# Two-layer gated MLP behind windowed attention on one core: layer 1's last 1024 tokens times w_out by seven block products, layer 2's w_in blocks stored in fp32

## The chip, the core and the metric

The kernel runs on one core of one Trainium2 chip. Time is what the device takes for one execution, in microseconds (us); several executions are timed and their median is given. The core's engines are TensorE (PE, the matrix engine; PEld is its weight load), the Vector engine (DVE), the Scalar engine (ACT), GpSimd (POOL) and SyncE (SP), which here issues nearly all DMA transfers. SBUF is the on-chip memory, PSUM holds what PE writes.

## The reference

2304 tokens pass through windowed attention (4 batches, 8 heads, 576 positions, head width 64, each query sees itself and the 63 keys before it) and then through two MLPs:

```python
x = attention(q, k, v)                       # (2304, 512)
h = x @ w_in1;  g = h - np.tanh(h)           # (2304, 2048)
x = (g @ w_out1).astype(np.float32)          # (2304, 512)
h = x @ w_in2;  g = h * (1.0 / (1.0 + np.exp(-1.702 * h)))
return (g @ w_out2).astype(np.float32)
```

The weights come as fp64; q, k and v as fp32. w_in is 512 x 2048, w_out 2048 x 512.

## The kernel before

**Accuracy.** Each fp64 weight is turned on chip into an fp32 number, and every fp32 operand of a product is split into a high half that PE's fp32r format holds exactly and a low half, the difference. A product is then three matmuls, hi x hi, hi x lo and lo x hi; the function `three` (L697) issues them. Multiplying one 128x128 weight tile so by 512 columns is 3 matmuls, and the weight loads go with them.

**Conversion.** A weight tile of 128x512 fp64 numbers is loaded as pairs of 32-bit words (`raw`). ACT takes the absolute value of the upper word (L305), DVE clamps it from below (L309), masks and shifts it (L312), puts in the bits of the lower word (L318) and the sign (L324); ACT writes the high half (L334), DVE the low half (L338). For layer 1 both halves stay in SBUF in one tile per f (f counts 16 columns of 128 of d_ff), w_in's part and w_out's side by side. For layer 2 `plan_wd` converts the tiles in pairs, POOL makes four sums S1 to S4 of their blocks (`wd_sums`, L380), ACT and DVE split plain blocks and sums alike (L384, L389), and both halves are stored to device memory (`wd_store`, L398): `wd` for w_in, `wdo` for w_out. They are fetched again later, as `ws` (`load_ws`, L440) and `wo` (`load_wo`, L444).

**Layer 1.** Tokens go in blocks of 512, 512, 256, 512 and 512 (0 to 4). For a block there are 16 steps h and 16 steps p, alternating with a lag of 2: step h (`hid`) multiplies x by one 128-column tile of w_in into the PSUM tile `psh` (4 x 3 = 12 matmuls, 512 columns each); ACT makes tanh and DVE subtracts (L723), ACT takes the high half gh and DVE the low half gl (L731); step p (`proj`) adds g times one row tile of w_out into four PSUM tiles `acc` (12 matmuls). At the end of a block the sums are evicted (`os`) and stored to device memory (`xs`), as layer 2 needs tokens in another grouping. Attention (L554 to L632) is spread over the first part of this.

**Layer 2.** Its first 256 tokens go the same way (a plain block). The other 2048 go in two units of 1024, u = 0 and 1, in which both matrix products are made with 7 block products in place of 8 (Winograd's form): sums and differences of blocks of the weights (S1 to S4) and of the activations (T1 to T4) are multiplied, and the seven products P1 to P7 are combined by additions on DVE. Tokens (two halves of 512) and the other side (pairs of tiles, j = 0 to 7) are the halves that the blocks are made from. The order of the products and the blocks that they take:

```python
PROD = dict(P1=(A11, "C11"), P5=(S1, "T1"), P6=(S2, "T2"), P7=(S3, "T3"), P2=(A12, "C21"), P3=(S4, "C22"), P4=(A22, "T4"))
OSEQ = (("P1", "P5", "P6", "P7", "P2", "P3", "P4"), ("P1", "P5", "P6", "P7", "P3", "P4", "P2"))
```

The gates of a unit lie in tiles `ug` (four parts of 512 columns per j: C11, C12, C21, C22); T1 to T4 are made from them by `u_sub` (L940, T1 on POOL, the others on DVE), split by `o_hi` (ACT, L950) and `o_lo` (DVE, L954) into gh and gl and multiplied with `ws` tiles into the PSUM tiles `ob` (`o_prod`). The unit's x side is `xt`, split into `xh`, `xl` or `xu` (L883, L890); `x2b` is the second partial of an x (L879).

**What sets the order.** No loop of the program is the order on the engines. Every piece of work is entered in a plan with its engine, an assumed duration, a due time (`prio`), what it waits for and which slots of a pool it takes and gives back (`raw` 3, `gp` 3, `psh` 2, `ws` 4, ...). `Plan.order` then plays through time and gives each free engine the ready piece that is due first; the instructions are written in that order and each engine runs its own in it, waiting where a semaphore is not there yet. `KNOBS` holds numbers that shift the due times of some kinds of work. SP's list is such an order too: a load or store whose data or slot is not ready holds back all that stand behind it on SP.

Of the kernel before, what the change touches and what calls it, by code (L numbers as in the profile page):

```python
# [24 lines left out]
class Plan:  # L25
# [127 lines left out]
    v=171.2,  # L153
# [9 lines left out]
    att=(6.1, 14.4),  # L163
    xu=35.8,
    wd=(235.4, 11.6, 283.0),
    seg=(4, 10),
    wds=4,
)
# [3 lines left out]
def attn_moe2_kernel(  # L172
# [75 lines left out]
    plan = Plan(dict(raw=3, cw=K["cw"], s=K["s"], psh=2, g=2, gp=3, kq=1, v=1, sa=K["sa"], x=2, acc0=1, acc1=1, acc2=1, acc3=1, a0=1, a1=1, ws=4, wds=K['wds']))  # L248
# [3 lines left out]

    steps = [(z, f) for z in turns for f in range(z[2], z[3])]
    seq = []
    for i in range(len(steps) + LAG):
        seq += [("h", steps[i])] if i < len(steps) else []
        seq += [("p", steps[i - LAG])] if i >= LAG else []
# [9 lines left out]
    for what, s in seq:  # L267
# [12 lines left out]
    wt = {}  # L280
    raw = {}
# [16 lines left out]
    def conv_abs(key):  # L298
        layer, f, i = key
        if layer == 1 and (layer, f) not in wt:  # L300
            wt[layer, f] = wp.tile([P, 2, 2, NB], F32R, tag=f"w{f}", name=f"w{f}")
# [21 lines left out]
    def conv_sign(key):  # L323
        nc.vector.scalar_tensor_tensor(  # L324
            out=bits[key], in0=raw[key][:, :, 1], scalar=0xC0000000, in1=bits[key],
            op0=ALU.bitwise_and, op1=ALU.bitwise_or,
        )

    def halves(key):
        layer, f, i = key  # L330
        return [wt[layer, f][:, i, j, :] for j in range(2)]
# [11 lines left out]
    def plan_w(key, d, after, gate=()):  # L343
# [7 lines left out]
        for fn, x in ((conv_clamp, 0.34), (conv_mant, 0.34), (conv_low, 0.6)):  # L351
# [30 lines left out]
    def wd_hi(j, m, i):  # L382
        o = stage[j, m, i, 0] = st.tile([P, NB], F32R, tag="s", name="wds")
        nc.scalar.activation(o, pair_of(j, m, i), AF.Copy)  # L384

    def wd_lo(j, m, i):
        x = pair_of(j, m, i)
        o = stage[j, m, i, 1] = st.tile([P, NB], F32, tag="s", name="wdl") if i < 2 else x
        nc.vector.tensor_tensor(out=o, in0=x, in1=stage[j, m, i, 0].bitcast(F32), op=ALU.subtract)  # L389

    def wd_store(j, m, i, b):
        if m == 0 and j not in wd:
            wd[j] = dr.tile([P, 2, 8, HB], F32, name=f"wd{j}")
        if m == 1 and "out" not in wd:
            wd["out"] = dr.tile([P, 2, 8, NJ, HB], F32, name="wdo")
        dst = wd[j][:, b] if m == 0 else wd["out"][:, b, :, j]
        x, y = (POS[z] for z in PAIRS[m][i])
        nc.sync.dma_start(out=dst[:, x : y + 1 : y - x], in_=stage[j, m, i, b].bitcast(F32).rearrange("p (k c) -> p k c", k=2))  # L398

    wd_done = {}  # L400

    def plan_wd(j, m, d, after):
        signs, ls, cs = [], [], []
        both = add({"SP": 1.2}, lambda _: [load_w((2, 2 * j + i, m)) for i in (1, 0)], d - 5, after, acq=("raw", "raw"), size=2 * P * NB * 8)
        for i in range(2):
# [7 lines left out]
            for fn, x in ((conv_clamp, 0.34), (conv_mant, 0.34), (conv_low, 0.6)):  # L413
# [5 lines left out]
        los, sts = [], []  # L419
        for i in range(4):  # L420
# [1046 lines left out]
```

## Time and profile before

| | |
|---|---|
| median of 3 runs | 849.46 us (848.4 to 850.03) |
| the profiled execution's own time | 849.77 us |
| span of its profile | 847.9 us |
| TensorE clock granted, mean | 0.997 of full |
| PE busy | 832.5 us, 5689 instructions |
| DVE / ACT / POOL busy | 605.0 / 434.0 / 153.9 us |
| read from device memory / written | 136.05 / 45.09 MB |

The span runs from the first to the last instruction of the profiled execution, the own time has what lies around it too. Busy is time in which an engine has an instruction in work; a matmul may be in work while it waits in PE's pipeline, so starts of consecutive matmuls give their pace, not the length of one. In 40 equal slices PE is at 0.9 or more in all but the first and the last; DVE's share, slice by slice in tenths, is 6999999888889898884233655343999744458964: high for the first 19 slices (400 us), and again between 590 and 680 us and near the end. Between them layer 1's last blocks (380 to 465 us), layer 2's plain block (465 to 530 us), unit 0's w_in products (to 605 us) and its w_out products (605 to 686 us) follow each other.

### The profile page before, as it was taken

The page shows a single profiled execution, that of the slowest core. Times are in us where ns is not written, and L with a number is a line of the kernel's source. Part 1 is how long each engine was busy: PE and PEld are TensorE (multiplying, and loading weights), DVE is VectorE, ACT ScalarE, POOL GpSimd, SP SyncE. Part 2 cuts the span into 40 slices and gives each one's busy share as a digit, 9 for nine tenths or more (in the row PEclk, how much of TensorE's full clock was granted, in tenths as well). Part 3 has the DMA queues.
Part 4 walks back from the last instruction along what each step waited for, and adds up shares of the span by engine and source line. Part 5 has one row for each costly group of instructions (what it writes and reads, how often), then busy time and mean ns, then how long its engine had stood idle before and what let it go on. Part 6 is the DMA issues. An engine that isn't in the chain of part 4 may idle for free.

```text
span 847.9 us, 15194 instructions
## 1 busy us (share of the span) xinstructions
PE 832.5 (98%) x5689; PEld 725.0 (86%) x5689; DVE 605.0 (71%) x1050; ACT 434.0 (51%) x997; POOL 153.9 (18%) x171
## 2 busy tenths in 40 slices
PE   8899999999999999999999999999999999999997
PEld 5798888888899987888888888888899988889997
DVE  6999999888889898884233655343999744458964
ACT  6887665556776757773222433323555522335443
POOL 3110000123111332120000000455500015552000
PEclk9999999999999999999999999999999999999999
DMA  9754455679879887862567696455757765566571
GB/s 330 267 159 151 151 169 191 196 261 296 272 255 290 280 278 253 282 212 99 177 214 231 185 285 186 150 173 191 272 196 245 217 209 174 180 211 245 164 235 60
DMA packets 106747, 182.15 MB, mean 215 GB/s; under 512 B 6704, under 2 KB 70192, under 8 KB 106672
## 3 DMA queue, kind: packets, MB, share of 16 engines
q1 hardware_dynamic: 106240, 180.64, 65.0%
q8 instruction: 45, 0.74, 0.4%
q10 hardware_dynamic: 432, 0.52, 0.2%
q14 instruction: 30, 0.25, 0.1%
HBM read 136.05 MB, written 45.09 MB: 214 GB/s over the span
## 4 chain that ended last, share of the span: by engine, by line
PE 87%; DVE 5%; ACT 5%; DMA 1%; issue 1%; SPq 0%; DVEq 0%; POOL 0%; ACTq 0%; POOLq 0%
PE psh L697 23%; PE acc L697 22%; PE ob L697 18%; PE m L697 18%; ACT s L591 3%; PE psa L632 2%; PE psa L559 2%; PE psa L615 1%; DMA raw<-in_w_in 1%; DMA xt<-xs 0%; PE wps L1011 0%; DVE s L608 0%; DVE xu L890 0%; DVE xt L883 0%; DVE g L723 0%
## 5 line engine op out<-in xcount | busy, mean ns | idle before, releaser
L697 PE MATMUL psh<-xh,w 128*128 128x512 f32 (+1 forms) x672 | 198.3, 362 | 0.0
L697 PE MATMUL acc<-gh,w 128*128 128x512 f32 (+1 forms) x672 | 198.0, 362 | 0.0
L697 PE MATMUL ob<-ws,gh 128*128 128x256 f32 x896 | 161.9, 283 | 0.0
L697 PEld LDWEIGHTS ob<-ws,gh 128*128 128x128 f32 x896 | 140.0, 192 | 0.2
L697 PEld LDWEIGHTS psh<-xh,w 128*128 128x128 f32 x672 | 121.5, 189 | 20.9 <-issue 1.5
L697 PEld LDWEIGHTS acc<-gh,w 128*128 128x128 f32 x672 | 121.6, 189 | 20.2 <-issue 0.7
L697 PE MATMUL ob<-ws,gl 128*128 128x256 f32 x448 | 126.9, 283 | 1.6 <-DVE gl L954 1.6
L697 PE MATMUL psh<-xl,w 128*128 128x512 f32 (+1 forms) x336 | 120.7, 359 | 0.0
L697 PE MATMUL acc<-gl,w 128*128 128x512 f32 (+1 forms) x336 | 120.7, 359 | 0.0
L937 POOL TENSOR_TENSOR ug<-ug,g 128x512 f32<-128x512 f32 x48 | 63.3, 1319 | 302.0 <-ACT g L933 300.9
L950 ACT ACTIVATE gh<-ug 128x512 fp32r<-128x512 f32 x112 | 70.4, 630 | 72.0 <-PE ob L697 67.2
L723 DVE TENSOR_TENSOR g<-psh,g 128x512 f32<-128x512 f32 (+1 forms) x100 | 57.8, 578 | 66.8 <-ACT g L717 56.0
L954 DVE TENSOR_TENSOR gl<-ug,gh 128x512 fp32r<-128x512 f32 x112 | 82.4, 737 | 27.9 <-ACT gh L950 26.2
L697 PE MATMUL m<-xu,ws 128*128 128x512 f32 x384 | 92.3, 389 | 0.0
L717 ACT ACTIVATE g<-psh 128x512 f32<-128x512 f32 (+1 forms) x84 | 44.8, 534 | 87.5 <-PE psh L697 87.5
L697 PEld LDWEIGHTS ob<-ws,gl 128*128 128x128 f32 x448 | 86.0, 192 | 2.0 <-DVE gl L954 1.8
L925 DVE TENSOR_TENSOR ug<-ug,m 128x512 f32<-128x512 f32 x80 | 54.9, 687 | 42.4 <-PE m L697 42.0
L697 PEld LDWEIGHTS m<-xu,ws 128*128 128x128 f32 x384 | 71.9, 188 | 14.9
L731 DVE TENSOR_TENSOR gl<-g,gh 128x512 fp32r<-128x512 f32 (+1 forms) x100 | 63.6, 637 | 20.9 <-ACT gh L727 19.9
L933 ACT ACTIVATE g<-ug 128x512 f32<-128x512 f32 x48 | 30.3, 632 | 89.4 <-DVE ug L925 89.4
L380 POOL TENSOR_TENSOR raw<-cw 128x256 f32<-128x256 f32 x32 | 27.3, 854 | 262.6 <-DVE cw L324 191.6
L727 ACT ACTIVATE gh<-g 128x512 fp32r<-128x512 f32 (+1 forms) x100 | 54.3, 544 | 37.1 <-DVE g L723 36.8
(111 smaller groups left out, 1270.7 us busy)
## 6 DMA issues: line engine op xcount, KB each, us to landing
ws<-wdo SPq DMA_DIRECT2D x28, 1024.0 KB, 5.3
ws<-wd SPq DMA_DIRECT2D x24, 1024.0 KB, 6.1
raw<-in_w_in SPq DMA_DIRECT2D x32, 512.0 KB, 4.8
raw<-in_w_out SPq DMA_DIRECT2D x32, 512.0 KB, 4.0
ws<-wd SPq DMA_DIRECT2D x16, 768.0 KB, 7.3
wdo<-wds SPq DMA_DIRECT2D x32, 256.0 KB, 3.6
wd<-wds SPq DMA_DIRECT2D x32, 256.0 KB, 4.0
wo<-wdo SPq DMA_DIRECT2D x8, 1024.0 KB, 5.2
```

Of the source, the lines that this page charges most:

```text
L380: nc.gpsimd.tensor_tensor(out=x[o], in0=x[a], in1=x[b], op=op)
L591: nc.scalar.activation(s[:, h, p, :], x[:, p, :], AF.Exp, bias=nm[:, h, p : p + 1], scale=scale, accum_out=sm[:, h, p : p + 1],)
L697: nc.tensor.matmul(ps, lhsT=a, rhs=b, start=first and i == 0, stop=last and i == 2, skip_group_check=onto)
L717: nc.scalar.activation(g, psh[s], AF.Tanh)
L723: nc.vector.tensor_tensor(out=g, in0=psh[s], in1=g, op=ALU.subtract if s[0][0] == 1 else ALU.mult)
L727: nc.scalar.activation(gh, g, AF.Copy)
L731: nc.vector.tensor_tensor(out=gl, in0=g, in1=gh.bitcast(F32), op=ALU.subtract)
L925: nc.vector.tensor_tensor(out=u_val(u, j, o), in0=u_val(u, j, a), in1=mb[u, j, n], op=ALU.add)
L933: nc.scalar.activation(g, u_sum(u, j, o), AF.Sigmoid, scale=BETA)
L937: eng.tensor_tensor(out=u_val(u, j, o), in0=u_sum(u, j, o), in1=ut[u, j, o, "g"], op=ALU.mult)
L950: nc.scalar.activation(gh, u_val(u, j, PROD[n][1]), AF.Copy)
L954: nc.vector.tensor_tensor(out=gl, in0=u_val(u, j, PROD[n][1]), in1=gh.bitcast(F32), op=ALU.subtract)
```

## The change

Layer 1's tokens 1280 to 2303 (blocks 3 and 4) no longer alternate steps h and p. All 32 steps h come in a row, their gates are kept in tiles `ug` that lie where the w_out halves lay, and then the product with w_out is made by seven block products as in layer 2 (`plan_out` with u = -1; a step is 2 halves of the output x 3 = 6 matmuls of 512 columns, 7 x 8 = 56 steps). For that the w_out halves of layer 1 are stored to a third array `wdo2` (`a_store`), fp32 tiles are made again from them (`rebuild`), S1 to S4 are made, split and stored as in layer 2, and all are fetched back in 14 tiles `w1` of 1 MB. A w_in tile and a w_out tile no longer share one SBUF tile, but two f of one matrix do, and the slots are listed (IN, OUT); the `wo` tiles, `ws` tiles and some `xu` tiles of layer 2 take other slots. Layer 2's w_in blocks are stored once, in fp32, fetched as `wr` into `raw` slots and split by ACT and DVE (`ws_hi`, `ws_lo`). In the conversion the absolute value is scaled by 2^-112, which puts the exponent where the shift wants it: the clamp goes, the shift needs no mask. Two P1 tiles of layer 2's w_out products lie in `cw` slots and no longer in a `raw` slot. Several numbers of `KNOBS` differ.

```diff
-    att=(6.1, 14.4),
-    xu=35.8,
-    wd=(235.4, 11.6, 283.0),
+    att=(42.0, 11.0),
+    xu=42.5,
+    wd=(275.7, 16.5, 39.8),
...
+    UN = turns[-3:-1]
...
+    lead = lagged([s for s in steps if s[0][0] == 1 and s[0] not in UN])
+    plain = lagged([s for s in steps if s[0][0] == 2])
+    hs = [("h", s) for s in steps if s[0] in UN]
+    outs = [("O", n, j) for n in OSEQ[0] for j in range(NJ)]
+    seq = lead[:-LAG]
+    for i in range(LAG):
+        seq += [hs[i], lead[i - LAG]]
+    seq += hs[LAG:] + outs[:-3] + plain[:1] + outs[-3:-1] + plain[1:2] + outs[-1:] + plain[2:]
...
+    IN = (0, 1, 2, 3, 8, 9, 10, 11)
+    OUT = (4, 5, 6, 7, 12, 13, 14, 15)
+    W1S, OU = IN[:3], IN[4]
+    XW = dict(T1=IN[3], T3=IN[5], B21=IN[6], B22=IN[7])
+    WS = (IN[2], OUT[0], OUT[1], IN[0])
+    WO = OUT[2:5] + IN[1:2] + OUT[5:] + IN[4:5]
...
-        nc.scalar.activation(bits[key].bitcast(F32), raw[key].bitcast(F32)[:, :, 1], AF.Abs)
-
-    def conv_clamp(key):
-        w = bits[key].bitcast(F32)
-        nc.vector.tensor_scalar(out=w, in0=w, scalar1=LEAST, scalar2=None, op0=ALU.max)
+        nc.scalar.activation(bits[key].bitcast(F32), raw[key].bitcast(F32)[:, :, 1], AF.Abs, scale=2.0**-112)
 
     def conv_mant(key):
-        nc.vector.tensor_scalar(
-            out=bits[key], in0=bits[key], scalar1=0x07FFFFFF, scalar2=3,
-            op0=ALU.bitwise_and, op1=ALU.logical_shift_left,
-        )
+        nc.vector.tensor_scalar(out=bits[key], in0=bits[key], scalar1=3, scalar2=None, op0=ALU.logical_shift_left)
...
+    def a_store(f, b):
+        x, y = (POS[z] for z in PAIRS[2][f % 2])
+        dst = wdo(2)[:, b, x : y + 1 : y - x, f // 2]
+        nc.sync.dma_start(out=dst, in_=halves((1, f, 1))[b].bitcast(F32).rearrange("p (k c) -> p k c", k=2))
+
+    def rebuild(j, i):
...
+        hi, lo = halves((1, 2 * j + i, 1))
+        nc.vector.tensor_tensor(out=x, in0=hi.bitcast(F32), in1=lo.bitcast(F32), op=ALU.add)
...
+        if m == 0:
+            for i in range(4):
+                sts.append(add({"SP": 0.6}, lambda _, i=i: wd_store(j, 0, i), d + 6 + 2 * i, signs[1 - i :][:1] if i < 2 else [sums], size=P * NB * 4))
...
+    def load_wr(key, src):
+        t = wraw[key] = cv.tile([P, 4, HB], F32, tag="raw", name="wr")[:, : src.shape[1]]
+        nc.sync.dma_start(out=t, in_=src)
+
+    def ws_hi(key):
+        x = wraw[key]
+        nc.scalar.activation(new_ws(key)[:, 0, : x.shape[1]], x, AF.Copy)
+
+    def ws_lo(key):
+        x = wraw[key]
+        t = wstream[key][:, :, : x.shape[1]]
+        nc.vector.tensor_tensor(out=t[:, 1], in0=x, in1=t[:, 0].bitcast(F32), op=ALU.subtract)
...
+    def gate2(s):
+        z, f = s
+        if (-1, f // 2) not in ut:
+            ut[-1, f // 2] = wp.tile([P, 4, NB], F32R, tag=f"w{OUT[f // 2]}", name="ug").bitcast(F32)
+        nc.vector.tensor_tensor(out=ut[-1, f // 2][:, 2 * (f % 2) + UN.index(z)], in0=psh[s], in1=gt[s], op=ALU.subtract)
+
+    def load_w1(key, k, b, q):
+        t = wstream[key] = wp.tile([P, 2, 4, HB], F32R, tag=f"w{W1S[k % 3]}", name="w1")
+        nc.sync.dma_start(out=t.bitcast(F32), in_=wdo(2)[:, :, POS[b], 4 * q : 4 * q + 4])
...
+        if u < 0:
+            for e in range(2):
+                c = slice(e * P, (e + 1) * P)
+                three(ob[u, n][e], wh[:, c], wl[:, c], *og[u, n, j], not onto and j == 0, j == NJ - 1, onto=onto)
+            return
...
+        tag = utag[s] = ("acc2", "acc3", "h", "h", "acc0", "acc1")[len(hseq) % 6]
```

PE in layer 1's last block, before: a step p of block 4 (its tiles `acc`) and the step h behind it (`psh`, with `xh` and `xl` the halves of x).

```order
L697 MATMUL acc_4896<-gh,w_224 128x512
L697 MATMUL acc_4896<-gl,w_224 128x512
L697 MATMUL acc_4896<-gh,w_224 128x512
L697 MATMUL psh<-xh,w_854 128x512
L697 MATMUL psh<-xl,w_854 128x512
L697 MATMUL psh<-xh,w_854 128x512 x2
L697 MATMUL psh<-xl,w_854 128x512
L697 MATMUL psh<-xh,w_854 128x512 x2
```

And in the changed kernel, where the last step h ends and the first step of P1 begins (`ob` is the product's PSUM tile, gh and gl the halves of a gate).

```order
L783 MATMUL psh<-xl,w 128x512
L783 MATMUL psh<-xh,w 128x512 x2
L783 MATMUL psh<-xl,w 128x512
L783 MATMUL psh<-xh,w 128x512
L783 MATMUL ob<-gh,w_4513 128x512
L783 MATMUL ob<-gl,w_4513 128x512
L783 MATMUL ob<-gh,w_4513 128x512 x2
L783 MATMUL ob<-gl,w_4513 128x512
L783 MATMUL ob<-gh,w_4513 128x512 x2
```

The steps p of these blocks are gone from between the steps h; the products stand behind the last step h, and read gates that were made up to 32 steps earlier.

DVE during block 4, before: a gate (L723) and its low half (L731) per step.

```order
L723 TENSOR_TENSOR g<-psh,g 128x512
L731 TENSOR_TENSOR gl<-g,gh 128x512
L723 TENSOR_TENSOR g<-psh,g 128x512
L731 TENSOR_TENSOR gl<-g,gh 128x512
L723 TENSOR_TENSOR g<-psh,g 128x512
L731 TENSOR_TENSOR gl<-g,gh 128x512
```

And in the changed kernel while the products P6 and P7 run (`u_sub` is L1040, `o_lo` L1053, L965 adds a second partial to an x of unit 0).

```order
L965 TENSOR_TENSOR xt<-xt,x2b 128x256
L1040 TENSOR_TENSOR ug<-ug 128x512
L1053 TENSOR_TENSOR gl<-ug,gh 128x512
L1040 TENSOR_TENSOR ug<-ug 128x512
L1053 TENSOR_TENSOR gl<-ug,gh 128x512
L1040 TENSOR_TENSOR ug<-ug 128x512
L1053 TENSOR_TENSOR gl<-ug,gh 128x512
L1040 TENSOR_TENSOR ug<-ug 128x512
L1053 TENSOR_TENSOR gl<-ug,gh 128x512
L1040 TENSOR_TENSOR ug<-ug 128x512 x2
```

DVE now has one or two operations per product step of PE: a low half each, and a difference of gates for the products that take T2, T3 or T4; work for layer 2 stands between them.

SP at layer 2's plain block, before: block 4's results are stored (`xs`), and the `wo` tiles are fetched in a row.

```order
L786 DMA xs_0_4888<-os 128x512 x4
L444 DMA wo<-wdo 128x8x256 x5
L805 DMA x_5085<-xs_0_954 128x256
L444 DMA wo<-wdo 128x8x256
L809 DMA x2b<-xs_4_2429 128x256
```

And in the changed kernel (`wr` is a w_in block of layer 2 in fp32, `xt` and `x2b` are loads of unit 0's x).

```order
L517 DMA wr<-wd_4423 128x1024
L530 DMA wo<-wdo_1956 128x8x256
L961 DMA x2b<-xs_4_2561 128x256
L961 DMA x2b<-xs_10_2997 128x256
L957 DMA xt<-xs_0_1834 128x256
L957 DMA xt<-xs_0_3956 128x256
L957 DMA xt<-xs_0_1834 128x256
L957 DMA xt<-xs_0_3956 128x256
L517 DMA wr<-wd_4524 128x1024
L957 DMA xt<-xs_0_942 128x256
L957 DMA xt<-xs_0_1834 128x256
L530 DMA wo<-wdo_1956 128x8x256
```

The `wo` tiles, six of which lie where gates were, now alternate with the `wr` tiles and with unit 0's x on SP.

## Rows read from the trace of the kernel before

**Rows 1.** The page's span and busy time, share and instructions of each engine.

```profile
span 847.9 us, 15194 instructions
...
PE 832.5 (98%) x5689; PEld 725.0 (86%) x5689; DVE 605.0 (71%) x1050; ACT 434.0 (51%) x997; POOL 153.9 (18%) x171
```

**Rows 2.** Chain that ended last, 150 to 156 and 500 to 503 us: start, us.

```profile
150.18 2.72 PE psh L697 x12
152.90 2.72 PE acc L697 x12
...
499.98 1.43 PE psh L697 x12
501.42 1.39 PE acc L697 x6
```

**Rows 3.** Stretches: PE, PEld, DVE, ACT, POOL busy (instructions), PEclk, DMA share, GB/s.

```profile
25.00:71.00 46.00, 42.43 (x546) 37.34 (x547) 43.53 (x91) 37.90 (x137) 5.78 (x14) 0.96 0.52 179
85.00:200.00 115.00, 115.00 (x513) 95.34 (x512) 104.64 (x190) 66.03 (x112) 13.41 (x16) 1.00 0.62 200
240.00:300.00 60.00, 58.52 (x593) 55.46 (x593) 54.26 (x109) 41.22 (x122) 13.51 (x16) 1.00 0.91 293
380.00:465.00 85.00, 85.00 (x404) 70.23 (x403) 28.70 (x43) 24.19 (x42) 3.23 (x4) 1.00 0.54 177
465.00:530.00 65.00, 64.72 (x374) 56.75 (x373) 36.95 (x77) 25.75 (x56) 0.00 (x0) 1.00 0.73 222
530.00:605.00 75.00, 75.00 (x344) 62.58 (x343) 36.10 (x51) 25.06 (x42) 38.28 (x29) 1.00 0.58 191
605.00:686.00 81.00, 79.36 (x653) 78.81 (x652) 70.03 (x108) 43.24 (x72) 4.63 (x3) 1.00 0.68 225
```

**Rows 4.** What PE waited for: us in total, times, longest.

```profile
PE psa L615 <- DVE s L608: 4.7, 5, 1.5
PE ob L697 <- DVE gl L954: 1.6, 1, 1.6
```

**Rows 5.** Timeline of DVE, 606 to 615 us: start, duration in us.

```profile
607.18 0.69 DVE L925 TENSOR_TENSOR ug<-ug,m 128x512 f32<-128x512 f32 x1
607.78 1.37 DVE L890 TENSOR_TENSOR xh<-xt,xh 128x512 fp32r<-128x512 f32 x1
...
610.79 1.77 DVE L883 TENSOR_TENSOR xt<-xt 128x512 f32<-128x512 f32 x1
612.48 0.68 DVE L954 TENSOR_TENSOR gl<-ug,gh 128x512 fp32r<-128x512 f32 x1
613.08 0.68 DVE L890 TENSOR_TENSOR xu<-xt,xu 128x512 fp32r<-128x512 f32 x1
```

**Rows 6.** Timeline of POOL over the same stretch.

```profile
607.31 3.00 POOL L937 TENSOR_TENSOR ug<-ug,g 128x512 f32<-128x512 f32 x2 [3.65 <-ACT g L933]
610.28 1.72 POOL L940 TENSOR_TENSOR ug<-ug 128x512 f32<-128x512 f32 x1
```

**Rows 7.** Groups by line and shape: busy us, mean ns of one, idle before.

```profile
L309 DVE TENSOR_SCALAR cw<-cw 128x512 f32<-128x512 f32 x64 | 26.6, 419 | 1.9 <-ACT cw L305 1.7
L380 POOL TENSOR_TENSOR raw<-cw 128x256 f32<-128x256 f32 x32 | 27.3, 854 | 262.6 <-DVE cw L324 191.6 <-ACT gh L727 16.9 <-DMA vt<-in_v 16.6
L389 DVE TENSOR_TENSOR wdl<-cw,wds 128x512 f32<-128x512 f32 x32 | 25.2, 788 | 3.5 <-ACT wds L384 3.5
L940 POOL TENSOR_TENSOR ug<-ug 128x512 f32<-128x512 f32 x16 | 22.4, 1400 | 0.0
```

**Rows 8.** Tile wo, its matmuls and its loads: ns min/median/max, first and last start.

```profile
L697 PE MATMUL acc<-wo,gh x64: 389/389/504, 486.7 to 533.1; 128*128 128x512 f32 x64
...
L444 SPq DMA_DIRECT2D wo<-wdo x8: 580/580/672, 406.0 to 444.1; - x8
```

**Rows 9.** DMA issues on the page: KB each, median us from issue to landing.

```profile
wdo<-wds SPq DMA_DIRECT2D x32, 256.0 KB, 3.6
```

**Rows 10.** Timeline of PE from 70 us: the first product of the ninth step.

```profile
70.81 0.50 PE L697 MATMUL psh<-xh,w 128*128 128x512 f32 x1
```

More of the change, by code (lines that the diff above doesn't have):

```diff
@@ L330, in halves @@
         layer, f, i = key
-        return [wt[layer, f][:, i, j, :] for j in range(2)]
+        return [wt[f // 2, i][:, f % 2, j] for j in range(2)]
     def conv_hi(key):
@@ L454, in w_into @@
             c = slice(kk * P, (kk + 1) * P)
-            return [wt[layer, f][:, 0, j, c] for j in range(2)]
+            return [x[:, c] for x in halves((layer, f, 0))]
         i = (A21 if kk < 2 else A22) if f % 2 else (A11 if kk < 2 else A12)
@@ L1180, in stream @@
-        after = after + ([last_proj[8 + n]] if n < NS else [])
-        streams[key] = add({"SP": 0.6}, lambda _: load_ws(key, src()), d - 14, after, acq=("ws",), size=P * (b - a) * NB * 4, behind=last[0])
-    for what, s in seq:
-        layer, f = s[0][0], s[1]
-        if layer == 2 and not wd_done:
-            last = None
-            for n in range(2 * NJ):
-                d = K["wd"][0] + K["wd"][1] * n
-                near = [made[x] for x in made if due["h", x] < d - 8]
-                last = plan_wd(n % NJ, 1 - n // NJ, d + K["wd"][2], near[-1:] + [last])
+            streams[key] = ws_own[key] = add(
+                {"SP": 0.6}, lambda _: load_ws(key, wdo(1)[:, :, POS[j], a:b]), d - 14, wd_done[1, NJ - 1] + after,
+                acq=("ws",), size=P * (b - a) * NB * 4, behind=last,
+            )
@@ new lines, in stream @@
+            return
+        k1 = (b - a) / 4
+        l = ws_raw[0] = add({"SP": 0.6}, lambda _: load_wr(key, wd[j][:, a:b]), d - 16, wd_done[0, j] + chain[-K["lag"][1] :][:1], acq=("raw",), size=P * (b - a) * HB * 4, behind=ws_raw[0])
+        h = ws_own[key] = add({"ACT": 0.1 + 0.9 * k1}, lambda _: ws_hi(key), d - 9, [l] + after, acq=("ws",), behind=last)
+        streams[key] = add({"DVE": 0.1 + 1.07 * k1}, lambda _: ws_lo(key), d - 9, [h], rel=[("raw", l)])
+    touch = {f: [] for f in range(KF)}
@@ new lines, in attn_moe2_kernel, with plan_gate @@
+    gate_of = {}
+    hseq = []
+    def plan_gate(s):
+        nonlocal prev
+        z, f = s
+        d = due["h", s]
+        t, j = UN.index(z), f // 2
+        tag = utag[s] = ("acc2", "acc3", "h", "h", "acc0", "acc1")[len(hseq) % 6]
+        t0 = blocks[1][z[1]][0]
+        xr = [x_ready[i] for i in range(t0 // P, t0 // P + 4)]
+        key = keys([tag])
+        prev = h = add(
+            {"PE": cost(s)}, lambda _: hid(s), d, [prev, converted[1, f, 0]] + xr,
+            acq=key, rel=[("x", x_owner[1, z[1]])] if f == KF - 1 else [],
+        )
+        hseq.append(h)
+        chain.append(h)
+        made[s] = h
+        a1 = add({"ACT": 0.5}, lambda _: gate1(s), d + 2, [h], acq=("g",))
+        a2 = add({"DVE": 0.6}, lambda _: gate2(s), d + 2, [a1] + [y for x in (f - f % 2, f - f % 2 + 1) for y in [last_proj[x]] + a_done[x]], rel=[(key[0], h), ("g", a1)])
+        touch[IN[j]].append(h)
+        touch[OUT[j]].append(a2)
+        g = gate_of.setdefault((-1, j), {})
+        g["C" + "12"[f % 2] + "12"[t]] = a2
+        if t and f % 2 == 0:
+            g["T1"] = add({"POOL": 1.25}, lambda _: u_sub(-1, j, "T1", "C12", "C11"), d + 4, [g["C11"], a2])
+            touch[OUT[j]].append(g["T1"])
@@ new lines, in attn_moe2_kernel @@
+    for what, s, *rest in seq:
+        if what == "O":
+            if (0, 0) not in wd_done:
+                last = None
+                for n in range(2 * NJ):
+                    d = K["wd"][0] + K["wd"][1] * n
+                    near = [made[x] for x in made if due["h", x] < d - 8]
+                    last = plan_wd(n % NJ, 1 - n // NJ, d + K["wd"][2], near[-1:] + [last])
+            plan_out(-1, s, rest[0], due[what, s, rest[0]])
+            continue
+        if s[0] in UN:
+            if not a_done:
+                plan_w1()
+            plan_gate(s)
+            continue
+        layer, f = s[0][0], s[1]
@@ L1247, in attn_moe2_kernel @@
     t = t_units
[L1248 to L1251 removed]
+    last_p0 = [s for what, s in plain if what == "p"][-2:]
     order = []
```

363 lines of the change are left out of this document (231 added, 132 removed).

## Prediction

> **What bounds the kernel now.** I read the page's busy lines first [rows 1]: TensorE (PE) is busy 832.5 of 847.9 us, the Vector engine (DVE) 605.0. A busy PE need not be a useful one, so the chain of waits comes next [rows 2]. From 85 us to 465 us it consists, apart from attention pieces, of two kinds of step: 12 products psh (x times w_in) and 12 products acc (g times w_out), 2.72 us each, one behind the other. 2.72 / 12 = 0.2267 us is the pace of a matmul with 512 columns. The table by stretches [rows 3] says the same from the other side: between 85 and 200 us and between 380 and 465 us PE has no idle time at all, while DVE is at 91% in the first of them and at 34% in the second. The list of PE's waits [rows 4] holds 4.7 us behind attention's DVE work and a single 1.6 us wait in a product of layer 2. So what is taken off PE comes off the time, as long as nothing new makes PE wait. Two places are close to that already: DVE (and, at the start, the Scalar engine ACT) before about 200 us, and the DMA engines at 0.91 of their time between 240 and 300 us [rows 3].
>
> **The change part by part.**
>
> *Layer 1's last 1024 tokens.* Before, blocks 3 and 4 (512 tokens each) need 16 acc steps each: 2 x 16 x 12 = 384 matmuls of 512 columns. Afterwards the same product is made as 7 products of half blocks, each 8 steps of 6 matmuls: 7 x 8 x 6 = 336. The x times w_in half (32 steps) is the same. 384 - 336 = 48 matmuls less, 48 x 0.2267 = 10.9 us off an engine that never waits there. This is the main term.
>
> *What the products need beside PE.* A product step is 6 x 0.2267 = 1.36 us of PE. For it ACT makes gh and DVE gl, and for 24 of the 56 steps DVE also subtracts two gate tiles. Between the first and the last gl of these products the new order has on DVE: 107 operations of 512 columns, which follow each other at 0.60 us (612.48, 613.08 in [rows 5]), 64.2 us; six additions of 256 columns and two operations with one input, taken at the clamp's 0.42 [rows 7], 3.4 us; four splits of 1024 columns, which no row shows: 1.2 us as an estimate, twice the 0.60; 4.8 us. Together 72.4 us against 56 x 1.36 = 76.2 us of PE: 95%. The nearest stretch of before is layer 2's first set of products: DVE 70.03 of 81 us, 86%, with the one wait of 1.6 us [rows 3, 4]. Taken: a wait of 1 us; bounds 0 and 6.5 (first rival).
>
> *Parts of w_out for it.* The halves of w_out are stored (32 stores of 256 KB, 32 more of the differences), S1 to S4 are made from them (16 additions on DVE, 32 more on POOL at 0.85 us [rows 7], 16 splits on ACT and DVE). In the new order they stand among the steps of blocks 1 to 4, beside PE's products. The gate of a pair of w_out blocks overwrites its tile, so it waits for the stores and for the rebuilding additions; behind it on DVE stand attention and other conversions. A 256 KB store takes 3.6 us to land [rows 9], and six banks of PSUM let PE run five steps, 13.6 us, ahead of a late gate. I take 0; bounds 0 to 3.
>
> *Conversions.* 64 clamps of 0.419 us go, and 32 of the 64 subtractions for layer 2's weights (0.788 the dearer kind) [rows 7]: 27 + at most 25 = 52 us less DVE work, nearly all beside a PE that is busy. Only before 71 us does PE wait for DVE and ACT: 12 clamps stand there, 12 x 0.42 = 5 us. But in the new order 130 DVE instructions stand before the ninth gate, where 133 stood: the clamps are gone, and one more conversion and pieces of attention have moved up into their place. That gate's products start at 70.8 us [rows 10]. I take 0, bounds -5 and +2.
>
> *Layer 2's w_in stored once.* 40 loads carry half the bytes, and 40 splits on ACT and DVE take their place, 24 of 1024 columns (1.2 us) and 16 of 768 (0.9): 43 us of DVE. Eight of the first kind stand in layer 2's first block, where DVE had 37 of 65 us; the rest in the stretches with 36 of 75 us [rows 3]. A sum that waits behind one is late by 1.2 us and is wanted only two products later, 2 x 1.36 us. 0.
>
> *w_out of layer 2.* Before, its eight 1 MB tiles were fetched from 406 to 444 us and first used at 486.7 us [rows 8]. In the new order six of their slots hold gates until the last product, so the first tile is fetched about five product steps (6.8 us) before layer 2's first block goes on alone, and the others while it runs. From that tile to the last SP's order holds 8 x 1,024 + 6 x 512 + 384 + 12 x 128 + 2 x 256 KB = 14.0 MB. The last tile is first used 6.8 + 16 x 1.43 + 14 x 1.39 [rows 2] + 5.4 us later (four products of layer 2 stand before the last two steps): 54.5 us, so 257 GB/s are wanted. The stretch from 240 to 300 us moved 293 GB/s for 60 us [rows 3]. I take 0.5 us of waits, bounds 0 and 19 (second rival).
>
> **Sum.** -10.9 + 1 + 0.5 = -9.4 us against the profiled execution's own 849.8 us (span 847.9 and 1.9 around it): 840.4. That execution lies 0.3 us above the median 849.46, so **840.0 us**.
>
> **A rule weighed against it.** DVE operations that read two tiles of SBUF lasted 1.37 and 1.77 us while POOL worked from 607.31 to 612.0 us, and 0.68 us right after; one that reads PSUM took 0.69 us [rows 5, 6]. The Trainium skill (SBUF — State Buffer, "SBUF: two separate sides") calls the ports that VectorE and GpSimd share an exclusive lock: the later one waits for the whole of the other's instruction. The trace agrees: the surplus, 1.09 us, is the rest of a POOL operation. By that rule POOL's additional 32 sums (0.85 us) and 8 differences (1.40 us, [rows 7]), 38.5 us, would be time in which DVE's two-input work stands still; only what falls on the products counts, and that is the first rival.
>
> **Rivals.**
> 1. *DVE paces the products.* If POOL's last group of sums and last two differences (6 operations) run beside the first products, each holds DVE for up to 1.09 us: 6.5 us, of which the 3.8 us of slack (76.2 - 72.4) hide some. For it: at 611 us PE waited for just this. Against it: in POOL's order all but that group stand behind gates that are made before the products begin. Loss 2.5 to 6.5 us instead of 1: 842 to 846, say **844**.
> 2. *Slower: layer 2's first block waits for its weights.* If the DMA engines deliver no more than the 191 GB/s of the stretch in which layer 2's tiles were streamed before (530 to 605 us, [rows 3]), the 14.0 MB take 73 us instead of 54.5: 19 us of waits at PE's acc<-wo, 849.8 - 10.9 + 19 - 0.3 = **858**. It decides against the change from 14.0 / (54.5 + 10.9) = 214 GB/s downwards; at the 222 GB/s of 465 to 530 us it would leave 847. For it: the tiles no longer come 40 us early. Against it: in those stretches the engines were at 0.58 and 0.73 of their time, so nothing more was asked of them.
> 3. *The start gains too.* If the 5 us of clamps before 71 us count in full, 840 - 5 = **835**. For it: DVE was busy 43.5 of 46 us there [rows 3]. Against: the order, above.
>
> **How the numbers follow.** Forecast 0.63, first rival 0.20, second 0.05, third 0.12. The forecast's own range is 837 to 842; with the third rival below and the first above it the range is **834.5 to 846**, and the second rival with the tails is left out. No change means within 0.2% (1.7 us) of 849.46, about what a measurement can tell. Faster: forecast, third rival and nearly all of the first, 0.93; slower 0.04, most of the second rival; same 0.03, from its lesser part and the first one's tail.
>
> **What would show it.** Right: 336 products ob of 512 columns with gh, gl in layer 1; psh steps at 2.72 us and product steps at 1.36 us without idle time between; a span near 838.5. The main term is wrong if the products' steps take over 1.36 us. First rival: PE waits for gl in the first ten product steps, with DVE operations of over 1.2 us beside POOL's. Second: PE waits for wo or ws in layer 2's first block while the DMA share is under 0.9. Third: the ninth psh step starts several us earlier. The forecast as a whole is wrong outside 837 to 842.

## The result

| | median (runs) | against before |
|---|---|---|
| before | 849.46 us (848.40 to 850.03, 5 runs) | |
| changed | 856.32 us (853.48 to 858.19, 5 runs) | ratio 1.0079, 95% interval 1.0054 to 1.0104 |

The change made the kernel 0.8% slower; the forecast was 840.0 us, 1.1% faster. The profiled execution of the changed kernel took 854.67 us, 4.9 us more than that of before; the medians are 6.9 us apart, and the other 2.0 us were not seen in a profile. Its span and busy line:

```profile
span 852.9 us, 15375 instructions
PE 822.5 (96%) x5639; PEld 715.5 (84%) x5639; DVE 679.1 (80%) x1085; ACT 469.8 (55%) x1040; POOL 213.9 (25%) x211
```

PE's busy time fell by 10.0 us [rows 1], near the main term's 10.9. The time was lost in idle PE. What PE waited for (us in total, times, longest), the three lines that matter:

```profile
PE ob L783 <- DMA w<-wdo: 12.3, 1, 12.3
PE psa L701 <- DVE s L694: 5.0, 5, 1.5
PE ob L783 <- DVE gl L1053: 1.9, 2, 1.7
```

The second and third are waits that the kernel before had too [rows 4], L694 and L1053 being its L608 and L954. The first is new: one wait of 12.3 us, in layer 1's products, for a tile `w1` of the w_out parts (the trace calls it `w`). Around it, in stretches (columns as in rows 3):

```profile
405.00:415.00 10.00, 10.00 (x46) 8.28 (x45) 10.00 (x18) 5.71 (x10) 8.41 (x1) 1.00 0.76 260
415.00:424.00 9.00, 8.97 (x40) 7.11 (x38) 9.00 (x16) 3.98 (x7) 9.00 (x1) 1.00 0.00 0
424.00:430.00 6.00, 0.00 (x0) 0.00 (x0) 2.06 (x4) 0.63 (x1) 4.72 (x4) 0.75 0.16 59
430.00:436.00 6.00, 0.00 (x0) 0.00 (x0) 0.00 (x0) 0.00 (x0) 0.00 (x0) 0.50 0.93 313
436.00:440.00 4.00, 3.71 (x9) 2.97 (x10) 0.12 (x1) 0.63 (x1) 0.00 (x0) 0.50 0.99 408
```

For 9 us before PE stops, the DMA engines move nothing, and POOL is busy all the time with one single instruction. The tile was not slow on its way; it was not sent. The chain of waits through the place (start, us, what) gives the order of events:

```profile
406.59 20.07 POOL raw L400
426.65 0.07 issue
426.72 2.09 POOL raw L400 x3
...
430.25 0.02 SPq L1029
430.27 0.03 issue
430.30 5.85 DMA w<-wdo
436.15 0.14 issue
436.29 13.87 PE ob L783 x51
```

The first of the four sums L400 of layer 2's last w_in group lasts 20.05 us, its three sisters 0.7 us each. DVE, over the same time (start, duration):

```profile
406.37 0.69 DVE L1053 TENSOR_TENSOR gl<-ug,gh 128x512 fp32r<-128x512 f32 x1
406.98 0.42 DVE L965 TENSOR_TENSOR xt<-xt,x2b 128x256 f32<-128x256 f32 x1
407.31 0.68 DVE L1040 TENSOR_TENSOR ug<-ug 128x512 f32<-128x512 f32 x1
...
425.37 0.69 DVE L1040 TENSOR_TENSOR ug<-ug 128x512 f32<-128x512 f32 x1
439.88 0.69 DVE L1053 TENSOR_TENSOR gl<-ug,gh 128x512 fp32r<-128x512 f32 x1 [13.82 <-ACT gh L1049]
```

These are 33 operations. Every one reads two tiles of SBUF, and each starts 0.60 us after the one before, though it lasts 0.68 or 0.69 (the one of 256 columns lasts 0.42, and the next starts 0.33 us after it): there is no moment without one between 406.37 and 426.06 us. POOL's addition ends at 426.64 us, 0.6 us after the run does. SP stands in order behind it:

```profile
407.98 0.53 SPq L1029 DMA_DIRECT2D w<-wdo  x1
427.47 1.73 SPq L433 DMA_DIRECT2D wd<-raw  x2
429.29 0.91 SPq L961 DMA_DIRECT2D x2b<-xs  x2
430.30 14.29 SPq L1029 DMA_DIRECT2D w<-wdo  x4
```

The two stores L433 store POOL's sums. Behind them stand two x loads and the sixth `w1` load. PE used up the five tiles that were there at 423.6 us and stopped; with PE stopped no tile for gate halves came free for ACT, DVE ran out of work at 426.06 us, and POOL's addition ended behind that.

The wait has a tail. The granted clock was 1.00 while PE worked, falls to 0.50 (1.2 of 2.4 GHz) while it stands, and ten steps between matmul starts take 4.39 us after it (436.29 to 440.68) where they take 2.27 at full clock: 2.1 us more. So 854.67 - 849.77 = 4.9 us is made of -10.9 (48 matmuls), +12.3 and +2.1, and +1.4 for the rest. The rest hides a loss at the start: PE is idle for 10.9 of the first 85 us, against 7.4 before, with a new wait of 1.6 us for DVE (`psh` for `xl`); 2.1 of these 3.5 us come back elsewhere.

### The profile page after: what moved, and what is told of

It reads as the page before. It is cut to its first block, busy times and chain, and to the rows that moved or that the text cites. A ratio compares the mean times of both kernels' runs of the same rounds, so it can differ in the third digit from the quotient of the medians.

```text
span 852.9 us, 15375 instructions
## 1 busy us (share of the span) xinstructions
PE 822.5 (96%) x5639; PEld 715.5 (84%) x5639; DVE 679.1 (80%) x1085; ACT 469.8 (55%) x1040; POOL 213.9 (25%) x211
## 4 chain that ended last, share of the span: by engine, by line
PE 77%; DVE 9%; DMA 4%; POOL 3%; ACT 3%; issue 2%; SPq 1%; DVEq 0%; ACTq 0%; POOLq 0%
PE ob L783 23%; PE psh L783 22%; PE m L783 17%; PE acc L783 12%; POOL raw L400 3%; PE psa L701 1%; PE psa L718 1%; DMA x2b<-xs 1%; PE psa L645 1%; DMA wo<-wdo 1%; DVE gl L1053 1%; ACT s L677 1%; DVE cw L337 1%; DVE s L694 1%; DMA w<-wdo 1%
## 5 line engine op out<-in xcount | busy, mean ns | idle before, releaser
L1049 ACT ACTIVATE gh<-ug 128x512 fp32r<-128x512 f32 x168 | 105.2, 629 | 110.3 <-PE ob L783 96.5
L1053 DVE TENSOR_TENSOR gl<-ug,gh 128x512 fp32r<-128x512 f32 x168 | 120.6, 721 | 42.8 <-ACT gh L1049 40.3
L400 POOL TENSOR_TENSOR raw<-cw 128x256 f32<-128x256 f32 x48 | 59.3, 1236 | 240.8 <-DVE cw L343 84.6
L783 PE MATMUL acc<-gh,w 128*128 128x512 f32 (+1 forms) x416 | 113.4, 344 | 0.0
L783 PE MATMUL ob<-gh,w 128*128 128x512 f32 x224 | 71.6, 398 | 12.4 <-DMA w<-wdo 12.3
L783 PEld LDWEIGHTS acc<-gh,w 128*128 128x128 f32 x416 | 73.6, 189 | 9.9 <-issue 0.9
L783 PEld LDWEIGHTS psh<-xl,w 128*128 128x128 f32 x336 | 63.5, 189 | 11.1 <-DVE xl L738 2.2
L783 PE MATMUL acc<-gl,w 128*128 128x512 f32 (+1 forms) x208 | 70.8, 340 | 0.0
L526 DVE TENSOR_TENSOR ws<-wr,ws 128x1024 fp32r<-128x1024 f32 (+1 forms) x40 | 53.6, 1343 | 10.3 <-ACT ws L521 10.0
L783 PEld LDWEIGHTS ob<-gh,w 128*128 128x128 f32 x224 | 43.0, 192 | 22.2 <-issue 12.7
L521 ACT ACTIVATE ws<-wr 128x1024 fp32r<-128x1024 f32 (+1 forms) x40 | 38.7, 969 | 41.4 <-PE m L783 33.0
```

The source lines that it names most:

```text
L400: nc.gpsimd.tensor_tensor(out=x[o], in0=x[a], in1=x[b], op=op)
L521: nc.scalar.activation(new_ws(key)[:, 0, : x.shape[1]], x, AF.Copy)
L526: nc.vector.tensor_tensor(out=t[:, 1], in0=x, in1=t[:, 0].bitcast(F32), op=ALU.subtract)
L783: nc.tensor.matmul(ps, lhsT=a, rhs=b, start=first and i == 0, stop=last and i == 2, skip_group_check=onto)
L1049: nc.scalar.activation(gh, u_val(u, j, PROD[n][1]), AF.Copy)
L1053: nc.vector.tensor_tensor(out=gl, in0=u_val(u, j, PROD[n][1]), in1=gh.bitcast(F32), op=ALU.subtract)
```

## The experiments

Theory A: as long as DVE's two-input SBUF operations follow each other without a break, POOL's addition is kept out; two stores that need its result then hold back `w1` loads on SP. The first two kernels ask when POOL is kept out, the others what that costs. Each ratio is against the kernel before on the same chip, with its 95% interval behind it.

**The port alone.** Two kernels that hold only small sections: a run of DVE operations, and one POOL addition of 128x256 whose input is DVE's third result.

> This kernel computes nothing of the reference; it is a row of small sections on VectorE (DVE) and GpSimd (POOL) alone. In each, DVE runs 8, 16 or 32 operations of 512 columns back to back and POOL has one addition of 128x256 whose input is the result of DVE's third operation. Theory A (DVE holds the port that both engines share as long as its two-input SBUF operations follow each other without a break): POOL's addition lasts 0.74 us plus what is left of DVE's chain, about 5 x 0.60 = 3 us in the section with 8, 8 us with 16, 17 to 18 us with 32. Theory B (the engines take turns, at most one operation each): under 2 us in all of them. With the rest of the chain reading PSUM in place of a second SBUF tile both expect under 1.5 us. In the sections with one other operation in the middle of 20, or a gap of about 1 us there, A expects that POOL comes in at that place (about 4 us) if the operation or gap lets the port go, and at the chain's end (about 10 us) if not; I expect the first for PSUM and the gap, and am open on the one-input operations. With POOL first, eight additions of 512 columns in a row, one DVE operation waits for the rest of one of them (up to 2 us) by both.

Beside a run that reads PSUM the addition took 0.73 us. With runs of two-input operations it took 8.33 us in the section with 16, to the run's end, but 1.10 us in those with 8 and 32: neither A nor B as they were put. Two inputs are not what it takes: a run of 13 one-input fp32 operations kept it out as well (4.87 us). A gap or a one-column operation in the middle ended the wait (4.12 us), a one-input fp32 operation there did not (10.47). With POOL first, the DVE operation beside its eight additions lasted 1.73 us; POOL's run did not keep DVE out for longer. Leaving out the run that reads PSUM, the sections differed in when the addition started behind the start of DVE's operation: 150 to 157 ns where it was kept out, 161 to 165 ns where it came in.

> Computes nothing of the reference: again sections of VectorE (20 operations of 512 columns each) beside one GpSimd addition of 128x256, eight kinds, each six times in turn. In the first such kernel the addition lasted either 1.1 us or as long as VectorE's unbroken run, and its start lay 162 to 165 ns behind the start of VectorE's operation in the first case and 150 to 157 ns in the second. Theory E (where in VectorE's operation the addition arrives decides): within each of the kinds with two-input SBUF operations both outcomes occur, split at about 160 ns, and nothing in between but in the kinds with a break. In the outcomes that are kept out: about 10.5 us with a one-input fp32 operation in the middle (no break), about 4.1 us with an operation of one column or a gap in the middle (a break), and, still open, 4 or 10 us with one operation that reads PSUM and one integer shift in the middle. The kind whose run reads PSUM: 0.7 us in all six. Rival F (the kind of operations in the section decides, each kind always the same).

The groups of POOL's additions by section, six each (busy us, mean ns of one):

```profile
L68 POOL TENSOR_TENSOR p_midone<-k_midone,b 128x256 f32<-128x256 f32 x6 | 62.5, 10417 | 67.5 <-DVE k_midone L35 67.5
L68 POOL TENSOR_TENSOR p_two<-k_two,b 128x256 f32<-128x256 f32 x6 | 54.5, 9079 | 44.5 <-DVE k_two L35 44.5
L68 POOL TENSOR_TENSOR p_one<-k_one,b 128x256 f32<-128x256 f32 x6 | 36.9, 6150 | 65.8 <-DVE k_one L35 65.8
L68 POOL TENSOR_TENSOR p_midgap<-k_midgap,b 128x256 f32<-128x256 f32 x6 | 24.4, 4064 | 45.8 <-DVE k_midgap L35 45.8
L68 POOL TENSOR_TENSOR p_midtiny<-k_midtiny,b 128x256 f32<-128x256 f32 x6 | 24.4, 4062 | 65.9 <-DVE k_midtiny L35 65.9
L68 POOL TENSOR_TENSOR p_midpsum<-k_midpsum,b 128x256 f32<-128x256 f32 x6 | 6.3, 1050 | 10.8 <-DVE k_midpsum L35 10.8
L68 POOL TENSOR_TENSOR p_psum<-k_psum,b 128x256 f32<-128x256 f32 x6 | 4.4, 728 | 20.2 <-DVE k_psum L35 20.2
```

`p_two` is five times 10.67 us and once 1.1; every other kind came out alike all six times, which is rival F's picture more than theory E's. The few ns of E are there, but not at 160 ns in all turns: in the later turns kept out at 217 to 223 ns, let in at 223 to 227; in the first turn kept out at 153 to 156, let in at 159 to 162 (the kind whose run reads PSUM left out: there POOL always came in). Up to the addition's start the kinds `two`, `midone` and `midpsum` are the same instructions, so what comes later in the run can't be why `midpsum` got in. Because the sections with a PSUM reader or a shift in the middle came in at once, whether these would let POOL in stays open.

That the arrival decides is not shown, though. In both small kernels the sections in which POOL came in are also those whose first DVE operation had to wait some 0.6 us or more for an input, and this sorts them without the tie at 223 ns. And the traces of the whole kernels speak against it. In the changed kernel the addition started 215 ns behind a DVE operation and was kept out. In the kernel before, one that started 216 ns behind came in after one operation, though DVE's next two-input SBUF operations followed without a gap. First POOL, then DVE:

```profile
303.89 1.06 POOL L380 TENSOR_TENSOR raw<-cw 128x256 f32<-128x256 f32 x1 [9.43 <-ACT gh L727]
```

```profile
303.68 0.69 DVE L389 TENSOR_TENSOR wdl<-cw,wds 128x512 f32<-128x512 f32 x1
304.28 1.23 DVE L731 TENSOR_TENSOR gl<-g,gh 128x512 fp32r<-128x512 f32 x1
305.43 1.23 DVE L389 TENSOR_TENSOR wdl<-cw,wds 128x512 f32<-128x512 f32 x1
```

So these runs show that a run can keep POOL out until it breaks, and not what decides whether it does.

**The four sums on DVE.**

```diff
-            nc.gpsimd.tensor_tensor(out=x[o], in0=x[a], in1=x[b], op=op)
+            (nc.vector if (j, m) == (NJ - 1, 0) else nc.gpsimd).tensor_tensor(out=x[o], in0=x[a], in1=x[b], op=op)
```

> Only the last four of the additions L400 (layer 2's last w_in group) run on VectorE in place of GpSimd; the order on every engine is otherwise the same. Theory A (GpSimd's addition is kept out for 20 us by VectorE's unbroken run of two-input operations; two stores that need it then hold back the w1 loads behind them on SyncE): no operation on GpSimd to be kept out, no wait for w1, no fall of TensorE's clock: 854.7 - 12.3 - 2.2 = 840 us, range 838.5 to 841.5. Rival B (the w1 tiles come too late in any case, being issued only when a slot is free and 1 MB long): a wait of 5 us or more at TensorE's ob<-w stays, 846 us or more. Rival C (VectorE is too full in the products, four more operations make it worse): waits for gl of 3 us or more, 843 us or more.

840.89 us (840.39 to 845.53), ratio 0.9909 (0.9893 to 0.9926). The wait for `w1` is gone from PE's list; its second line is now

```profile
PE ob L783 <- DVE gl L1053: 2.8, 3, 1.7
```

of which 0.9 us at 410 us stands behind the four sums. The sixth `w1` load goes out at 414.60 us, 15.7 us earlier than in the changed kernel. A's number; B and C are out.

**POOL keeps its sums, the stores stand elsewhere.** On SP the two stores go behind five `w1` loads:

```diff
-        got = plan.order()
+        got = later(plan.order())
+    late = [t for t in got if t.get("tag") == "last sums"]
+    got = [t for t in got if t.get("tag") != "last sums"]
+    here = next(i for i, t in enumerate(got) if t.get("tag") == 9) + 1
+    return got[:here] + late + got[here:]
```

> GpSimd keeps its additions; the two stores that wait for the last of them are moved on SyncE behind five w1 loads, nothing else is moved. Theory A: GpSimd's first addition of that group still lasts 15 us or more (VectorE's run is the same), but the w1 loads are no longer behind it: no wait of over 1 us for w1, 840 us, range 838.5 to 842. Rival B (w1 late in any case): 846 us or more with the wait still there. Rival D (GpSimd's addition is long because SyncE or the DMA engines hold it up): it is short, about 0.74 us, as soon as the stores stand elsewhere.

842.07 us (840.09 to 844.38), ratio 0.9913 (0.9896 to 0.9930), 0.1 us over the range given, and no wait for `w1`. POOL's addition, though:

```profile
408.03 20.06 POOL L400 TENSOR_TENSOR raw<-cw 128x256 f32<-128x256 f32 x1 [10.06 <-DVE cw L343]
```

So the 20 us are not SP's or the DMA engines' doing, and cost PE nothing by themselves. What cost 14 us (12.3 and 2.1) was the place of two stores in SP's list. Rivals B and D are out. What let the addition end was a DVE operation that started 0.06 us late, 0.66 us behind the one before it in place of 0.60. The meeting of the two engines has a price of its own, but a small one: when the addition has ended, POOL's other three sums and DVE's operations take turns, and PE waits 1.05 us for a low half at 432 us. It is in this line of PE's list, beside 1.7 us in layer 2:

```profile
PE ob L783 <- DVE gl L1053: 2.9, 3, 1.7
```

**One DVE operation of one column.** Everything stays in its place; one operation on 128x1 is put into DVE's run.

```diff
+    gap["fn"] = lambda _: nc.vector.tensor_scalar(out=scr, in0=ident[:, :1], scalar1=1.0, scalar2=None, op0=ALU.add)
+    return got[: b + 1] + [gap] + got[b + 1 :]
```

> The changed kernel, all sums on GpSimd and every store and load in its place, with one more VectorE operation: one column of a constant, four low halves of gates behind the place where the last group's sums are entered. Theory A, with what the small kernels showed (an operation of one column lets GpSimd in): the first addition lasts no longer than to that place, 3 to 6 us in place of 20, the other three about 1.1 us each; the stores and the w1 loads behind them go 14 us earlier, no wait for w1 of over 1 us: 839.5 to 842. If an unbroken run of two-input operations is not the cause, or the place is too early: 20 us again and 853 to 858.

POOL's sums, and DVE at that place:

```profile
406.32 6.22 POOL L400 TENSOR_TENSOR raw<-cw 128x256 f32<-128x256 f32 x1 [8.85 <-DMA wd<-cw]
412.62 1.07 POOL L400 TENSOR_TENSOR raw<-raw,cw 128x256 f32<-128x256 f32 x1
```

```profile
411.86 0.15 DVE L1680 TENSOR_SCALAR scr<-ident 128x1 f32<-128x1 f32 x1
411.92 2.32 DVE L1040 TENSOR_TENSOR ug<-ug 128x512 f32<-128x512 f32 x2
```

The addition ends at 412.54 us, 0.7 us behind the start of the one-column operation, and for the next three sums the two engines take turns; PE waits 1.0 us for a low half behind that, at 415 us. The wait for `w1` is gone: 843.40 us (841.31 to 843.50), ratio 0.9929 (0.9916 to 0.9943). The mechanism is as put; the median is 1.4 us over the range given. The profiled execution was the one of 841.31, so what the other four have more was not seen.

**Clamps.** What the conversion's removed clamps are worth, in three runs: put back as a maximum with zero into the changed order (with the sums on DVE), for all 64 tiles and for layer 1's 32; and left out of the kernel before.

```diff
+        w = bits[key].bitcast(F32); nc.vector.tensor_scalar(out=w, in0=w, scalar1=0.0, scalar2=None, op0=ALU.max)
         nc.vector.tensor_scalar(out=bits[key], in0=bits[key], scalar1=3, scalar2=None, op0=ALU.logical_shift_left)
```

> As e1_sums_dve, and each of the 64 weight tiles' conversions has one more VectorE operation of one input (a maximum with zero, which changes no value) where the clamp was; nothing else is moved. If clamps cost nothing after the start and their 12 before 71 us count in full: 5 us over e1_sums_dve, 845. If the waits there end at other things, as predicted: within 2 us of it, 840 to 842. If VectorE's 95% in the products of layer 1 is the limit, the clamps that stand there (four or so) bring waits for gl of 1 to 2 us there.

> As the run with all 64 clamps put back into the changed order, but only for layer 1's 32 tiles. That run had 5 to 6 us more idle time of TensorE before 80 us and 8 us more between 120 and 160 us, where layer 1's tiles are converted and layer 2's not yet: if those are the clamps of layer 1, 853 to 856. If the cost comes from layer 2's tiles (their conversions stand among attention and the rebuilt w_out parts), under 846.

> The kernel before with the changed conversion alone: the absolute value scaled, no clamp, no mask; its order on every engine is that of before with the 64 clamps left out. If the clamps stand beside a busy TensorE, as the prediction held: 847 to 849.2, the gain only from waits before 71 us. If VectorE's time before 200 us is the limit (16.7 us of the 17.2 us that the clamps cost in the changed kernel's order): 840 or less.

All 64: 858.10 us (857.59 to 858.67), ratio 1.0104 (1.0091 to 1.0117), 17.2 us over the run without them, against the 0 to 5 expected. Layer 1's alone: 855.37 us (855.08 to 856.30), ratio 1.0075 (1.0062 to 1.0088), 14.5 us, as its expectation had it. Left out of the kernel before: 847.06 us (845.88 to 847.20), ratio 0.9970 (0.9958 to 0.9981), 2.1 us, as expected if the clamps stand beside a busy PE. One saving, two prices. The stretch from 85 to 200 us shows a part of why; first the changed kernel, then the one with layer 1's clamps put back:

```profile
85.00:200.00 115.00, 115.00 (x566) 94.86 (x565) 103.18 (x171) 67.82 (x128) 22.30 (x25) 1.00 0.83 268
```

```profile
85.00:200.00 115.00, 109.51 (x509) 89.43 (x508) 103.08 (x180) 62.25 (x107) 18.90 (x22) 0.99 0.74 239
```

The changed kernel has DVE busy for 103.18 us there without the clamps, as before with them (104.64, [rows 3]): the 10.9 us of the 26 clamps that stood there went, by DVE's groups in the stretch, to additions of the w_out parts (4.0 us), more splits (3.8 us) and more pieces of attention (2.8 us). With the clamps on top PE loses 5.5 us in this stretch. DVE is at 90% in both, so it is not that it is full: PE stands still in three places, the two longest of them behind ACT's eviction and behind DVE's gate, for each of which conversions are first in the engine's order (at 149 and 143 us).

```profile
PE acc L784 <- ACT os L863: 3.3, 1, 3.3
PE psh L784 <- DVE g L811: 1.7, 1, 1.7
```

Of the other 9 us, 3.7 are more idle PE before 85 us, and 4.5 are longer busy time: between 25 and 71 us the granted clock is 0.94 in place of 1.00. The order of the changed kernel was laid out for the lighter conversion, so these are prices of work that its plan does not know of; what clamps cost in a plan that knows of them, no run shows.

**Mending it further.** Two kernels with the four sums on DVE but later, behind the second product's last low half. The first also moves unit 1's x preparation in layer 2 behind eight low halves of gates:

```diff
+    move(lambda t: t.get("tag") in (("sums", 7, 0), "last sums"), None, ("lo", -1, "P5", 7))
+    move(lambda t: t.get("tag") == ("xu", 1), ("lo", 0, "P1", 0), ("lo", 0, "P1", 7))
```

> The changed kernel with the last group's four sums on VectorE, but behind the low half of the second product's last step, and the two stores behind them; and in layer 2's first w_out product unit 1's x preparation (3 subtractions or sums and 4 low halves on VectorE, their high halves on ScalarE) moved behind the first eight low halves of gates. By theory A no wait for w1; the waits for gl near 409 us (1.1 us) and 603 us (1.8 us) go, and 1 us or so may come back where the moved work lands: 838.5 us, range 837 to 840.5, against 840.9 with the sums on VectorE alone. If the moved work is late for unit 1's first products instead: waits there of 1 us or more, 840 to 842.

851.26 us (848.30 to 853.67), ratio 1.0025 (1.0011 to 1.0040): a miss, and the same kind of mistake as the change's. The profile is of its fastest execution, 848.30 us. SP's loads of unit 1's x went with the work and came to stand behind loads of `ws`; DVE waited in order for them, and PE for what stood behind on DVE:

```profile
609.19 1.42 DVE L969 TENSOR_TENSOR xt<-xt 128x512 f32<-128x512 f32 x2 [6.51 <-DMA xt<-xs]
```

```profile
PE ob L783 <- ACT gh L1049: 8.6, 1, 8.6
```

The second leaves the loads alone and instead takes the last four POOL operations of unit 0 to DVE:

```diff
-        eng = nc.vector if o == "C11" else nc.gpsimd
+        eng = nc.vector if o == "C11" or (u, j) == (0, NJ - 1) else nc.gpsimd
-        (nc.gpsimd if o == "T1" else nc.vector).tensor_tensor(out=u_val(u, j, o)
+        (nc.gpsimd if o == "T1" and (u, j) != (0, NJ - 1) else nc.vector).tensor_tensor(out=u_val(u, j, o)
```

> The changed kernel with the last group's four sums on VectorE behind the low half of the second product's last step, their two stores behind them; and of layer 2's unit 0 the last pair's three gate products and one difference on VectorE in place of GpSimd. SyncE's loads of unit 1's x stay in their place. No wait for w1; the waits for gl near 409 us (1.1 us) go, the one near 603 us (1.8 us) falls by about 1 us, since VectorE's operations there no longer last 1.4 to 1.8 us but it has four more of 0.6 us: 839 us, range 838 to 841, against 840.9. If VectorE is too full there: 1 to 2 us more wait for gl, 841 to 843.

839.26 us (838.21 to 841.00), ratio 0.9887 (0.9870 to 0.9903), as expected: faster than both kernels, by 1.1% and 2.0%. The waits for gl, 2.8 us with the sums alone on DVE, are down to

```profile
PE ob L783 <- DVE gl L1053: 0.6, 2, 0.4
```

and the one near 603 us is gone, four more operations on DVE notwithstanding.

## Why the prediction was wrong, step by step

**The step that failed** is the wait in the products, taken at 1 us with bounds 0 and 6.5, and the first rival and the rule behind it, from which the upper bound comes. It asked what POOL's last sums would cost DVE ("each holds DVE for up to 1.09 us") and not what DVE's run would cost POOL. It had the place right (the last group, beside the first products), it had DVE at 95% there, and it priced the meeting at 2.5 to 6.5 us. The rows on which it rested [rows 5, 6] show POOL with three operations in a row and DVE coming to it. Where POOL came second in the kernel before, it waited for one operation (1.06 us at 303.9 us), so no longer wait stood there to be read. In the products POOL waited not for one operation but for all 32 that followed in the run: 20.05 us. PE lost 12.3 us by it, and 2.1 more to the clock. Where POOL did get its turn beside the products, in the runs with the stores moved and with the one-column operation, the meeting cost PE 1.0 us, less than the rival's 2.5. The Trainium skill (SBUF — State Buffer, "SBUF: two separate sides") has the first to start hold the pair for its whole instruction and the other wait fully. The trace agrees that it is exclusive; that the wait always ends with one instruction it does not bear out: 20.05 us against DVE instructions of 0.69.

**The queue behind it** was not asked for at all. The step on w_out's parts and that on layer 2's w_in named who waits on DVE, but not what stands on SP behind stores that wait for POOL. The second rival had PE wait for streamed weights, in another place (layer 2's plain block) and for another reason (bandwidth). There the DMA engines delivered 321 GB/s, where 257 were wanted and 222 had been moved before [rows 3], and PE lost next to nothing (nor does PE wait for `wo` or `ws` in the run with the sums on DVE, in which nothing stalls ahead of this block):

```profile
465.00:530.00 65.00, 64.69 (x374) 56.60 (x373) 49.38 (x86) 37.48 (x69) 0.00 (x0) 1.00 0.96 321
```

**The main term** held: PE's busy time fell by 10.0 us, though 2.1 us at the low clock are in it, and by 11.7 us with the sums on DVE. Without the stall the kernel gains 8.3 us (849.21 to 840.89) with 0.9 us of new wait from the sums on DVE, 9.7 us with the last mend (848.92 to 839.26). The forecast's sum was -9.4. That the first of these comes so near is in part luck: a loss of 3 us at the start, which the sum did not have, is in it, and PE's busy time fell by more than the sum's 10.9.

**The wait of 1 us in the products**, the part of it that is for gl, was 0.2 us in the changed kernel beside the stall (1.9 us for gl, 1.7 of them in layer 2), 1.1 to 1.3 us in the first three runs without the stall, and 0.6 with the last mend. DVE did keep pace with PE.

**Conversions** were taken at 0, between -5 and +2. In the kernel before, leaving the clamps out gave 2.1 us. The rest of their 27 us bought no time by itself, as forecast, but in the changed order it was needed: with layer 1's clamps back that order loses 14.5 us, while the prediction took the w_out parts, which now stand in the clamps' place, as free on their own.

**The third rival**, a faster start, did not come: between 25 and 71 us PE was busy for 41.0 us, against 42.4 [rows 3], and the waits behind attention stayed (5.0 us, [rows 4]: 4.7). The start lost 3.5 us instead, as said above, which no term of the sum had beyond +2; which part of the new order makes it no run separates.

**The chances** gave "slower" 0.04, all of it to a rival of bandwidth. The time lies 10 us above the range's upper end.

## What to carry to other kernels

Where VectorE is to be filled to 95% with operations that read two SBUF tiles (or, in the small kernels, one-input fp32 operations), look at what GpSimd does at that time and follow its results to whoever waits for them: its next operation may last as long as the run does. On a queue that works in order, a store that needs a slow engine's result belongs behind the loads that a busy engine wants soon; the slow operation and its sisters cost some 1 us once its stores stood there. A break in the run, here one operation of one column, is a cheap cure: 843.40 us in place of 856.32.

## What the runs showed of the hardware

A GpSimd addition of 128x256 that takes 0.73 us alone took 20.05 us beside a run of VectorE operations of 0.69 us (33 of them, one of 0.42), with no failure of any kind to see but its length. A run of 13 one-input fp32 operations kept one out too (4.87 us), a run that reads PSUM did not (0.73 us). What decides whether it is kept out is open: additions that started 215 to 219 ns behind the start of a VectorE operation were kept out beside layer 1's products, and one that started 216 ns behind was let in after one operation (1.06 us) in the kernel before. An operation of one column (0.15 us) or a gap ended the wait within 0.7 us, and in one kernel so did an operation that started 0.06 us late; an fp32 operation with one input in the middle did not. Once GpSimd was in, the two took turns, 1.1 to 1.2 us each. After 12 us without work TensorE's granted clock stood at 0.50, and it was back at full some 4.4 us after work began again.
